# Phase 1 of an adaLN block on one Trainium2 core: the transpose of x moved from TensorE to DMA and GpSimd, for token pairs 2 to 7

## The chip, the core and the metric

The kernel runs as one launch on one core of a Trainium2 chip. The core has a matrix engine (TensorE; PE in the profile, with its weight loads listed apart as PEld), three engines for elementwise work (VectorE or DVE, ScalarE or ACT, GpSimd or POOL), a queue engine that only starts transfers (SyncE or SP), and 16 DMA engines that all queues share. Every engine works through its own list of instructions in order, and engines wait for one another at semaphores. The metric is the time of one execution on the device in microseconds (us).

## The reference

The reference is one transformer block with adaptive layer norm, float32, sequence 2048, width 640, 32 heads of 20, hidden width 1728:

```python
mod = (_silu(c) @ w_mod).reshape(1, 6, 1, -1)
sa, ca, ga, sb, cb, gb = (mod[:, i] for i in range(6))
h = _layernorm(x) * (1 + ca) + sa
q, k, v = split(h @ wqkv)
phi(u) = concat(softmax(u @ w_phi), softmax(-(u @ w_phi)))       # per head, u = q or k
o = phi(q) @ (phi(k).T @ v) / (phi(q) @ sum(phi(k)) + 1e-6)
x = x + ga * (o @ wo)
h = _layernorm(x) * (1 + cb) + sb
x = x + gb * (relu(h @ w1 + b1) ** 2 @ w2 + b2)
```

## The kernel before

**Tiles and phases.** The 2048 tokens are 16 tiles of 128, taken as 8 pairs: pair j holds tiles 2j and 2j+1. Phase 1 makes k, v and q of every tile and sums phi(k)ᵀv; phase 2 forms the attention output and multiplies by `wo`; phase 3 is the two-layer feed-forward part. The change is in phase 1 alone.

**What a pair needs.** A projection contracts over the 640 features, so the normalized x of a pair must stand with features on partitions: five columns of 128 features (`d` = 0 to 4), each 128 partitions by 256 tokens. `ln_parts` normalizes the pair in place in its tile `xb` in three steps, between which it yields: sums (ScalarE, two passes, and a small GpSimd operation), squares (ScalarE, two passes into the scratch rows `junk`, and three small GpSimd operations), and scaling (ScalarE, two passes). Then `t1` turns the columns: two TensorE transposes of 128 by 128 per column into the PSUM tile `ta` (`t_in`), and `t_out`: ScalarE applies the modulation to give `hf`, ScalarE copies `hf` rounded to the high part of `hT`, and VectorE subtracts to give the low part. Every float32 product is made of three rounded ones, high by high, high by low, low by high (`three`). So a column is usable by its first two matmuls once ScalarE has written the high part, and by its third once VectorE has written the low part.

**One pair on TensorE.** For each tile: the projection to k (30 matmuls: 15 into a 384-wide bank, then 15 into a 256-wide one, columns 0 to 4 in order in each), to v, to q. At the even tile, after v, `do_kv` adds the products of the two tiles before. The turning of pair j+1 is spread over pair j: columns 0 and 1 at the end of the even tile (`t1(j + 1, 0, 1)`), columns 2 and 3 after v of the odd tile, and column 4 inside the q projection of the odd tile, where for three pairs a transpose for the modulation vectors (`mod_turn`) also stands. The k projection of the next pair follows at once. Tiles 12 to 15 have no q projection in this loop, so the last pairs are close together: pair 6 is first used at tile 12.

**What sets the order.** In this loop only TensorE's order is written by hand (`manual_schedule(engines={PE})`). The lists of ScalarE, VectorE, GpSimd and SP come out of a scheduler that estimates when operands will be there; `issue_after` adds single constraints. The order so made is fixed in the program. The list of SP holds the loads of x (`load_x`), the rows of `w_mod` (`wm`) and `wo` (`rwo`), and the stores `esp` of each tile's exponentials of q.

**Shared buffers.** `row("s3", ...)` gives rows from three buffers in turn: `junk` of the squares and `hf` of every column come from it. Four banks of PSUM (`pj`) hold the projections, two per projection, so TensorE can run about one projection ahead of ScalarE's copies out of PSUM. The rows k and q come from two buffers (`s2`).

Of the kernel before, what the change touches and what calls it, by code (L numbers as in the profile page):

```python
# [9 lines left out]
F32R = mybir.dt.float32r  # L10
I32 = mybir.dt.int32
AF = mybir.ActivationFunctionType
ALU = mybir.AluOpType
AX = mybir.AxisListType

P = 128
# [5 lines left out]
NT = S // P  # L22
NC = D // P
# [28 lines left out]
def kernel(  # L52
# [19 lines left out]
    nc = tc.nc  # L72
# [258 lines left out]
    def ln_parts(xt, nm, spare=None):  # L331
# [15 lines left out]
        for i in range(2):  # L347
            nc.scalar.activation(xt[:, i], xt[:, i], AF.Identity, bias=nb[:, i : i + 1], scale=sq[:, i : i + 1])
        yield

    def layer_norm(xt, nm, spare=None):
# [30 lines left out]

    def t1(j, *ds, more=None):
        if 0 in ds:
            HT[j] = ht(f"hT{j}", j)
        p = tp(f"ta{j}_{ds[0]}")
        for k, d in enumerate(ds):
            t_in(XB[j], d, p[:, 256 * k : 256 * k + 256])
        if more:
            mod_turn(more[0], p[:, 256:], 4)  # L390
        for k, d in enumerate(ds):
            t_out(cols_a, HT[j], d, f"a{j}", p[:, 256 * k : 256 * k + 256])
        DONE[:] = newest(ET_.Activation), newest(ET_.DVE)
        if more:
            mod_sum(*more)
# [317 lines left out]
    for t in range(2, NT - 2):  # L713
# [8 lines left out]
        if norm:  # L722
            if not i:
                parts = ln_parts(XB[norm], f"a{norm}")
            with tc.issue_after(newest(ET_.Activation)):
                next(parts)
        p = proj("v", t, (1, 0, lambda: t1(j + 1, 4)) if t == NT - 3 else None)
        if i == 0:
            do_kv(t - 2)
            do_kv(t - 1)  # L730
            if t in AFTER_KV:
                AFTER_KV[t]()
        v_out(t, p)
        if norm and not i:
            next(parts)
        EK[t] = tok2("k", f"ek{t}")
        spread(PK[t], EK[t], f"k{t}")
        exps(EK[t])
        if norm and not i:
            next(parts)  # L740
        if i and t < NT - 4:
# [3 lines left out]
        if t < NT - POSTPONED:  # L745
            do_q(t, (1, 3, lambda: t1(j + 1, 4, more=LAST_COL.get(t))) if i else None)
            if norm and i:
                with tc.issue_after(newest(ET_.Activation)), tc.issue_after(DONE[0]):
                    next(parts)
            if i:  # L750
# [4 lines left out]
        if i == 0 and t < NT - 4:  # L755
            t1(j + 1, 0, 1)
        if t == NT - 6:
            parts = ln_parts(XB[j + 2], f"a{j + 2}")
            with tc.issue_after(newest(ET_.Activation)):
                next(parts)  # L760
# [942 lines left out]
```

## Time and profile before

| | |
|---|---|
| median of the runs (lowest, highest) | 766.53 us (766.48, 767.01) |
| profiled execution, its own time | 766.05 us |
| its span | 764.3 us |
| TensorE matmuls busy | 758.5 us (99%) |
| TensorE weight loads busy | 739.7 us (97%) |
| VectorE, ScalarE, GpSimd busy | 593.9, 435.6, 144.9 us |
| granted TensorE clock | 1.0 throughout |
| phase 1's loop over tiles 2 to 13 | about 52 to 224 us |

The profile's page gives busy time by engine; the chain that ended last follows the work back from the last instruction; groups give count, busy time and mean length by line and operand names; windows give the engines' busy time in a stretch; the timeline lists instructions by start, with what ended the idle time before them. Line numbers are those of the kernel before (L357 is `t_in`, L368 and L369 are `hf` and the high part of `hT`, L88 the subtraction, L337, L342 and L348 are sums, squares and scaling, L338 and L343 to L345 GpSimd's small operations).

### The profile page before, as it was taken

Reading aid. Unit: us, or ns where it says so; the run is one execution under the profiler, and the core shown is the slowest. Engines: PE = TensorE matmul, PEld = TensorE weight load, DVE = VectorE, ACT = ScalarE, POOL = GpSimd, SP = SyncE. Lnnn points to the kernel's source line nnn. Section 1 sums busy time; section 2 is a strip of 40 time slices with the busy share of each in tenths; the row PEclk is TensorE's granted clock in tenths of the full one; section 3 lists DMA queues with packets and bytes.
Section 4 is the critical chain, followed back from the end, with each engine's and each line's share of the span. In section 5 each row is a group of like instructions: output and inputs, shape, how many; then the busy total and the mean of one; then the engine's idle time right before and its main releaser. Section 6 shows DMA issues by size and latency. Waiting matters only on the chain.

```text
span 764.3 us, 15303 instructions
## 1 busy us (share of the span) xinstructions
PE 758.5 (99%) x5968; PEld 739.7 (97%) x5968; DVE 593.9 (78%) x1083; ACT 435.6 (57%) x972; POOL 144.9 (19%) x301
## 2 busy tenths in 40 slices
PE   9999999999999999999999999999999999999997
PEld 8999999999999989988999999999999999999997
DVE  6598897988999899999655667876767666685666
ACT  5766756677853364546776647465563645536331
POOL 3001101001100255432101000231321313213110
PEclk9999999999999999999999999999999999999999
DMA  8811431343332345223366466996766759767460
GB/s 322 329 61 78 138 104 54 104 136 112 126 104 93 109 150 188 72 87 104 122 194 221 120 227 236 283 334 209 224 166 207 232 179 268 199 184 204 126 184 35
DMA packets 51505, 126.69 MB, mean 166 GB/s; under 512 B 6684, under 2 KB 7457, under 8 KB 51433
## 3 DMA queue, kind: packets, MB, share of 16 engines
q1 hardware_dynamic: 34098, 84.65, 32.8%
q0 software_dynamic: 14752, 35.76, 16.9%
q10 hardware_dynamic: 2583, 5.30, 1.8%
q8 instruction: 47, 0.77, 0.5%
q14 instruction: 25, 0.20, 0.1%
HBM read 95.70 MB, written 29.89 MB: 164 GB/s over the span
## 4 chain that ended last, share of the span: by engine, by line
PE 91%; DVE 7%; DMA 1%; issue 0%; SPq 0%; ACT 0%; DVEq 0%
PE up L78 24%; PE acc L78 18%; PE pq L78 9%; PE pk L78 9%; PE pv L78 9%; PE pwo L78 6%; PE acc3x L78 5%; PE kvp L450 3%; PE te L920 1%; DVE dn L878 1%; DVE scr L876 1%; DVE ezb L900 1%; PE tb L357 1%; PE ta L357 1%; DVE ot L88 1%; PE foldq L280 1%
## 5 line engine op out<-in xcount | busy, mean ns | idle before, releaser
L78 PE MATMUL up<-h,w 128*128 128x256 f32 x1640 | 206.4, 278 | 0.0
L78 PEld LDWEIGHTS up<-h,w 128*128 128x128 f32 x1640 | 196.1, 188 | 0.0
L1255 ACT ACTIVATE ft<-up,b_t 128x256 f32<-128x256 f32 x104 | 49.1, 472 | 113.8 <-PE up L78 113.2
L78 PE MATMUL acc<-w,ra 128*128 128x384 f32 x452 | 97.4, 335 | 0.0
L1256 DVE TENSOR_TENSOR ft<-ft 128x256 f32<-128x256 f32 x104 | 44.1, 424 | 48.4 <-ACT ft L1255 46.8
L78 PE MATMUL pwo<-wo,ot 128*128 128x256 f32 (+3 forms) x512 | 80.5, 312 | 0.1
L78 PEld LDWEIGHTS pwo<-wo,ot 128*128 128x128 f32 (+1 forms) x512 | 74.4, 188 | 3.2 <-issue 2.7
L78 PE MATMUL pq<-wq,hT 128*128 128x384 f32 (+1 forms) x480 | 75.2, 312 | 0.0
L78 PEld LDWEIGHTS acc<-w,ra 128*128 128x128 f32 x452 | 72.7, 188 | 0.8 <-DVE ra L88 0.5
L78 PE MATMUL pk<-wk,hT 128*128 128x384 f32 (+1 forms) x480 | 72.7, 308 | 0.0
L78 PE MATMUL pv<-wv,hT 128*128 128x384 f32 (+1 forms) x480 | 71.7, 307 | 0.0
L78 PEld LDWEIGHTS pq<-wq,hT 128*128 128x128 f32 x480 | 71.1, 188 | 0.6 <-issue 0.2
L78 PEld LDWEIGHTS pk<-wk,hT 128*128 128x128 f32 x480 | 70.5, 188 | 0.4 <-issue 0.2
L78 PEld LDWEIGHTS pv<-wv,hT 128*128 128x128 f32 x480 | 70.1, 188 | 0.0
L88 DVE TENSOR_TENSOR ra<-ft,ra 128x384 fp32r<-128x384 f32 (+2 forms) x86 | 36.8, 449 | 32.6 <-ACT ra L1279 19.3
L1365 POOL DMA_DIRECT2D ring_a<-td_a x34 | 18.3, 539 | 126.1 <-PE acc L78 100.4
L1279 ACT ACTIVATE ra<-ft 128x384 fp32r<-128x384 f32 x48 | 25.2, 526 | 28.4 <-DVE ft L1256 22.4
L78 PE MATMUL acc3x<-w,ra 128*128 128x256 f32 x231 | 39.8, 278 | 0.0
L78 PEld LDWEIGHTS acc3x<-w,ra 128*128 128x128 f32 x231 | 37.2, 188 | 0.2 <-DVE ra L88 0.2
L1270 DVE TENSOR_TENSOR ft<-ft 128x128 f32<-128x128 f32 x136 | 33.4, 287 | 1.2
L441 DVE TENSOR_REDUCE sk<-ek 128x64 f32<-128x1280 f32 x16 | 23.7, 1484 | 12.4 <-ACT ek L436 10.8
L884 POOL TENSOR_TENSOR dn<-dn,rs_q 128x32 f32<-128x32 f32 x32 | 20.2, 630 | 66.7 <-DVE dn L878 66.4
(270 smaller groups left out, 1412.6 us busy)
## 6 DMA issues: line engine op xcount, KB each, us to landing
ring_c<-td_c POOLq DMA_DIRECT2D x34, 384.0 KB, 4.2
ring_a<-td_a POOLq DMA_DIRECT2D x34, 384.0 KB, 4.1
ring_b<-td_b POOLq DMA_DIRECT2D x34, 256.0 KB, 4.0
esp<-eq SPq DMA_DIRECT2D x12, 640.0 KB, 3.0
el<-esp SPq DMA_DIRECT2D x12, 640.0 KB, 3.9
rw<-in_w SPq DMA_DIRECT2D x23, 320.0 KB, 2.9
wm<-in_w_mod SPq DMA_DIRECT2D x20, 320.0 KB, 3.3
xb<-in_x SPq DMA_DIRECT2D x8, 640.0 KB, 4.2
```

The costliest lines, as they stand in the source:

```text
L78: nc.tensor.matmul(o, a, b, start=first and i == 0, stop=last and i == len(terms) - 1, skip_group_check=skip,)
L88: (eng or nc.vector).tensor_tensor(out_lo, full, hi.bitcast(F32), op=ALU.subtract)
L280: nc.tensor.matmul(p[g // 3][:, (g % 3) * 120 : (g % 3) * 120 + n], r, bd_t[:120, g * 120 : g * 120 + n], start=True, stop=True,)
L357: nc.tensor.transpose(p[:, i * P : (i + 1) * P], xn[:, i, d * P : (d + 1) * P], ident)
L441: nc.vector.tensor_reduce(s, heads(flat(e)), axis=AX.X, op=ALU.add)
L450: nc.tensor.matmul(kvp[g // 4][64 * c : 64 * c + 64, a : a + 2 * n].rearrange("p (s n) -> p s n", s=2), v[:, u], e[:, :, o : o + n], start ...
L884: nc.gpsimd.tensor_tensor(dn[:, s], dn[:, s], rs[:, 1 - s], op=ALU.mult)
L1255: nc.scalar.activation(r, p, AF.Relu, bias=b1_t[:, f : f + 1])
L1256: nc.vector.tensor_tensor(r, r, r, op=ALU.mult)
L1270: nc.vector.tensor_tensor(t[:, o], t[:, a], t[:, b], op=op)
L1279: nc.scalar.activation(a[:, 0, :3], t[:, :3], AF.Copy)
L1365: nc.gpsimd.dma_start(RING[j, n, r], TD[n][r].bitcast(F32R))
```

## The change

For pairs 2 to 7 the TensorE transposes of `t1` go. In their place `by_dma`, called at the end of the scaling step, treats the pair's tile as 16-bit halves: GpSimd copies (`tensor_copy`, every second 16-bit element) make for each of the two token tiles a plane `pl` of low halves and one of high halves, four copies of 128 by 640; the two planes of a token tile lie in one `s3` row. SP then starts four transposing transfers (`dma_start_transpose`), one for each plane, which write back over the tile `xb`. In `t1` GpSimd joins the two halves of a column, two strided copies of 128 by 256, into the row `hf`; from there `t_out` goes on as before, with `hf` in SBUF in place of `ta` in PSUM. Every edit follows from this but two: the transpose of `mod_turn` stands ahead of the columns and has a PSUM tile of its own, and the steps of `ln_parts` are called earlier in the program text (for pairs 3 to 6 the sums at the end of the odd tile before, the squares after k of the even tile, the scaling before the copies of v).

```diff
         for i in range(2):
             nc.scalar.activation(xt[:, i], xt[:, i], AF.Identity, bias=nb[:, i : i + 1], scale=sq[:, i : i + 1])
+        if nm[0] == "a":
+            by_dma(int(nm[1:]), xt)
         yield
+
+    TURNED = {}
+
+    def by_dma(j, xt):
+        raw = flat(xt).bitcast(U16)
+        halves = raw.rearrange("p (i d h) -> p i h d", i=2, h=2)
+        turned = raw.rearrange("p (h b t) -> p h b t", h=2, b=NC)
+        planes = [row("s3", f"pl{j}_{i}").bitcast(U16).rearrange("p (h d) -> p h d", h=2) for i in range(2)]
+        for i in range(2):
+            for h in range(2):
+                nc.gpsimd.tensor_copy(planes[i][:, h], halves[:, i, h])
+        for i in range(2):
+            for h in range(2):
+                nc.sync.dma_start_transpose(turned[:, h, :, i * P : i * P + P], planes[i][:, h])
+        TURNED[j] = turned
...
     def t1(j, *ds, more=None):
+        if more:
+            mod_turn(more[0], tp(f"mc{j}")[:, 256:], 4)
         if 0 in ds:
             HT[j] = ht(f"hT{j}", j)
-        p = tp(f"ta{j}_{ds[0]}")
-        for k, d in enumerate(ds):
-            t_in(XB[j], d, p[:, 256 * k : 256 * k + 256])
-        if more:
-            mod_turn(more[0], p[:, 256:], 4)
-        for k, d in enumerate(ds):
-            t_out(cols_a, HT[j], d, f"a{j}", p[:, 256 * k : 256 * k + 256])
+        for d in ds:
+            hf = row("s3", f"hfa{j}_{d}")[:, :256]
+            for h in range(2):
+                nc.gpsimd.tensor_copy(hf.bitcast(U16).rearrange("p (t h) -> p h t", h=2)[:, h], TURNED[j][:, h, d])
+            t_out(cols_a, HT[j], d, f"a{j}", hf, hf)
...
         if norm:
-            if not i:
+            if t == 2:
                 parts = ln_parts(XB[norm], f"a{norm}")
+                next(parts)
             with tc.issue_after(newest(ET_.Activation)):
                 next(parts)
...
                 AFTER_KV[t]()
+        if norm:
+            next(parts)
         v_out(t, p)
-        if norm and not i:
-            next(parts)
...
         exps(EK[t])
-        if norm and not i:
-            next(parts)
...
-            if norm and i:
-                with tc.issue_after(newest(ET_.Activation)), tc.issue_after(DONE[0]):
-                    next(parts)
...
-        if t == NT - 6:
+        if (i and t < NT - 5) or t == NT - 6:
             parts = ln_parts(XB[j + 2], f"a{j + 2}")
             with tc.issue_after(newest(ET_.Activation)):
                 next(parts)
```

Since the scheduler sets the lists of the other engines, the change moves more than its lines say. Three places follow; in the names the first number is the pair (`hT6`, `hfa6_2` is column 2 of pair 6) or the tile (`q11`, `pq11_1` its second bank).

ScalarE, before, at the end of tile 11, ahead of pair 6's first use at tile 12:

```order
L426 ACTIVATE q11_2562<-pq11_0_2520 128x384
L306 ACTIVATE mt4_2313<-ta6_4_2540 128x128
L368 ACTIVATE hfa6_4_2545<-ta6_4_2540,cols_a_100 128x256
L369 ACTIVATE hT6_2389<-hfa6_4_2545 128x256
L426 ACTIVATE q11_2562<-pq11_1_2521 128x256
L348 ACTIVATE xb7_2215<-xb7_2215,nba7_2405,sqa7_2404 128x640 x2
L426 ACTIVATE k12_2577<-pk12_0_2578 128x384
```

The same place after:

```order
L444 ACTIVATE q11_2612<-pq11_1_2571 128x256
L387 ACTIVATE hT6_2429<-hfa6_1_2436 128x256
L338 ACTIVATE xb7_2251,sma7_2442<-xb7_2251 128x640 x2
L518 ACTIVATE wo2_2452<-rwo2_2448 128x640
L343 ACTIVATE junka7_0_2491,sqa7_2443<-xb7_2251,sma7_2442 128x640
L343 ACTIVATE junka7_1_2493,sqa7_2443<-xb7_2251,sma7_2442 128x640
L349 ACTIVATE xb7_2251<-xb7_2251,nba7_2444,sqa7_2443 128x640 x2
L386 ACTIVATE hfa6_2_2554<-hfa6_2_2554,cols_a_100 128x256
L387 ACTIVATE hT6_2429<-hfa6_2_2554 128x256
L386 ACTIVATE hfa6_3_2560<-hfa6_3_2560,cols_a_100 128x256
L387 ACTIVATE hT6_2429<-hfa6_3_2560 128x256
L386 ACTIVATE hfa6_4_2593<-hfa6_4_2593,cols_a_100 128x256
```

Before, all five columns of pair 6 are written ahead of the copy of the second q bank; now columns 1 to 4 stand behind it, and columns 2 to 4 also behind all three steps of pair 7's normalization and a piece of the `wo` weights.

GpSimd, before, at pair 7's normalization:

```order
L489 MEMSET rwo4_2718 128x640
L338 TENSOR_SCALAR sma7_2403<-sma7_2403 128x2
L343 TENSOR_SCALAR sqa7_2404<-sqa7_2404 128x2
L344 TENSOR_TENSOR sqa7_2404<-sqa7_2404,mhalf_96 128x2
L345 TENSOR_TENSOR nba7_2405<-sma7_2403,sqa7_2404 128x2
L503 DMA wo5_2820<-wo5_2820 40x640
```

The same place after:

```order
L339 TENSOR_SCALAR sma7_2442<-sma7_2442 128x2
L344 TENSOR_SCALAR sqa7_2443<-sqa7_2443 128x2
L345 TENSOR_TENSOR sqa7_2443<-sqa7_2443,mhalf_96 128x2
L346 TENSOR_TENSOR nba7_2444<-sma7_2442,sqa7_2443 128x2
L363 COPY pl7_0_2532<-xb7_2251 128x640 x2
L363 COPY pl7_1_2533<-xb7_2251 128x640 x2
L409 COPY hfa6_2_2554<-xb6_1885 128x256 x2
L409 COPY hfa6_3_2560<-xb6_1885 128x256 x2
L409 COPY hfa6_4_2593<-xb6_1885 128x256 x2
```

The joins of pair 6's columns 2 to 4 stand behind the four splits of pair 7. The rows `hfa6_3` and `hfa6_4` also take the `s3` buffers of `pl7_0` and `pl7_1`, so their joins wait until pair 7's transposing transfers have read these planes.

ScalarE, before, around the q projection of tile 5, ahead of pair 3's first use at tile 6:

```order
L436 ACTIVATE ek5_1421<-ek5_1421 128x640
L437 ACTIVATE ek5_1421<-ek5_1421 128x640
L426 ACTIVATE q5_1485<-pq5_0_1446 128x384
L368 ACTIVATE hfa3_4_1469<-ta3_4_1466,cols_a_100 128x256
L369 ACTIVATE hT3_1330<-hfa3_4_1469 128x256
L426 ACTIVATE q5_1485<-pq5_1_1447 128x256
```

The same place after:

```order
L444 ACTIVATE q5_1499<-pq5_0_1461 128x384
L386 ACTIVATE hfa3_0_1348<-hfa3_0_1348,cols_a_100 128x256
L444 ACTIVATE q5_1499<-pq5_1_1462 128x256
L387 ACTIVATE hT3_1347<-hfa3_0_1348 128x256
L386 ACTIVATE hfa3_1_1354<-hfa3_1_1354,cols_a_100 128x256
L387 ACTIVATE hT3_1347<-hfa3_1_1354 128x256
L386 ACTIVATE hfa3_2_1445<-hfa3_2_1445,cols_a_100 128x256
L387 ACTIVATE hT3_1347<-hfa3_2_1445 128x256
L386 ACTIVATE hfa3_3_1451<-hfa3_3_1451,cols_a_100 128x256
L387 ACTIVATE hT3_1347<-hfa3_3_1451 128x256
L386 ACTIVATE hfa3_4_1481<-hfa3_4_1481,cols_a_100 128x256
L387 ACTIVATE hT3_1347<-hfa3_4_1481 128x256
```

Before, four columns are done ahead of the q projection's copies and the fifth between them; now the high parts of all five stand behind the copy of the second q bank. In the other pairs the columns whose high part stands behind that copy are 3 and 4 (pair 2), 2 to 4 (pair 4), and 1 to 4 (pair 5); of pair 7 none. On SP the four transposing transfers of pairs 3 and 5 are parted after the second by the store of the even tile's exponentials of q; those of the other pairs follow one another. On VectorE the low parts of the columns stand ahead of the odd tile's row sums of exp(k) and its q work.

More of the change, by code (lines that the diff above doesn't have):

```diff
@@ L11 @@
 I32 = mybir.dt.int32
+U16 = mybir.dt.uint16
 AF = mybir.ActivationFunctionType
```

## The prediction

> **What bounds the kernel now.** I read the page's busy times first, then windows by stage, then the chain inside phase 1.
>
> ```profile
> PE 758.5 (99%) x5968; PEld 739.7 (97%) x5968; DVE 593.9 (78%) x1083; ACT 435.6 (57%) x972; POOL 144.9 (19%) x301
> ...
> 82.00:112.00 30.00, 30.00 (x237) 29.78 (x236) 27.01 (x36) 19.75 (x45) 2.84 (x4) 1.00 0.35 114
> 203.00:232.00 29.00, 29.00 (x231) 28.75 (x230) 27.30 (x37) 16.66 (x37) 0.00 (x0) 1.00 0.32 110
> 232.00:253.00 21.00, 21.00 (x196) 20.10 (x197) 19.64 (x23) 7.97 (x20) 0.77 (x1) 1.00 0.32 99
> 253.00:350.00 97.00, 96.69 (x716) 86.52 (x713) 93.51 (x138) 49.34 (x111) 44.02 (x88) 1.00 0.38 125
> ```
>
> The windows give PE, PEld, DVE, ACT and POOL in this order. In phase 1 (the first two rows) TensorE never stops and loads weights 99% of the time, so what leaves its list is won, and what it waits for is lost. VectorE is busy 27.0 of 30 us. From 253 to 350 us VectorE is the fuller one (93.5 of 97), so a delay handed to it there isn't made up.
>
> The chain through one pair (tiles 4 and 5, from 81.95 to 111.77) is TensorE alone:
>
> ```profile
> 81.95 4.30 PE pk L78 x30
> 93.03 4.58 PE pq L78 x30
> 97.60 0.44 PE ta L357 x4
> 98.04 4.38 PE pk L78 x30
> 106.72 0.43 PE ta L357 x4
> 107.16 2.98 PE pq L78 x18
> 110.13 0.22 PE ta L357 x2
> 110.35 1.42 PE pq L78 x12
> ```
>
> **Part 1, the transposes removed.** 0.44 + 0.43 + 0.22 = 1.09 us of the path in each pair, 6.5 us in six. The groups bound it from above:
>
> ```profile
> L357 PEld LDWEIGHTS ta<-ident,xb 128*128 128x128 f32 x60 | 7.0, 141 | 0.1
> L357 PE MATMUL ta<-ident,xb 128*128 128x128 f32 x60 | 9.5, 273 | 0.0
> ```
>
> I take the chain's 6.5; the matmuls' 9.5 overlap their neighbours and are the upper end. `mod_turn`'s transposes only move.
>
> **Part 2, the columns of hT arrive late.** TensorE wants all five columns when the q projection of the odd tile ends; call that moment T. By ScalarE's list they now stand behind the copy of the second q bank, which can't begin before T. The durations:
>
> ```profile
> 98.99 0.72 ACT L369 ACTIVATE hT<-hfa 128x256 fp32r<-128x256 f32 x2
> 111.80 0.39 ACT L426 ACTIVATE q<-pq 128x256 f32<-128x256 f32 x1 [0.36 <-PE pq L78]
> 201.72 0.56 ACT L368 ACTIVATE hfa<-ta,cols_a 128x256 f32<-128x256 f32 x1
> 202.31 0.42 ACT L369 ACTIVATE hT<-hfa 128x256 fp32r<-128x256 f32 x1
> 202.83 0.41 DVE L88 TENSOR_TENSOR hT<-hfa,hT 128x256 fp32r<-128x256 f32 x1
> ```
>
> The copy begins 0.05 after T, and the next instruction 0.45 after T. From `hf` to its `hT` 0.59 passes, from `hT` to the next instruction 0.36 (two in 0.72): 0.95 for a column. From the start of `hT` until VectorE has the low part 0.52 + 0.41 = 0.93. TensorE uses column 4's low part in its 15th matmul, 14 × 0.166 = 2.3 us after T (2.98 for 18). So with columns n to 4 behind the copy, the last low part is there at 0.45 + 0.36 + (4 − n − 1) × 0.95 + 0.59 + 0.93 for n below 4, and the wait is what exceeds 2.3:
> - pair 2 (n = 3): 2.33, no wait. Pair 4 (n = 2): 3.28, 1.0 us. Pair 5 (n = 1): 4.2, 1.9 us. Pair 3 (n = 0): 5.2, 2.9 us.
>
> In pairs 3 and 5 the last two transposing transfers also stand on SP behind a store that waits for exponentials:
>
> ```profile
> 93.25 1.74 ACT L348 ACTIVATE xb<-xb,nba,sqa 128x640 f32<-128x640 f32 x2 [0.95 <-POOL nba L345]
> ...
> 105.07 0.33 SPq L480 DMA_DIRECT2D esp<-eq  x1
> 143.91 0.38 SPq L328 DMA_DIRECT2D gate<-gate_a  x1
> 154.18 0.34 SPq L329 DMA_DIRECT2D ga_b<-gate  x1
> ...
> xb<-in_x SPq DMA_DIRECT2D x4, 640.0 KB, 4.0
> ...
> rwo<-in_wo SPq DMA_DIRECT2D x10, 150.0 KB, 2.6
> ```
>
> No row shows a transposing transfer. It moves 160 KB in short pieces. Low end: 2.6 us to landing, as the 150 KB loads. High end: the column of 4-byte pieces (`gate`), whose reader went out 10.3 us later. I take 5.0, nearer the low end because the bytes are those of the low row, and above the 640 KB row because four follow one another. The last of them goes out at 105.07 + 2 × 0.33 and lands at 110.75; a join (below) ends at 111.15. T is now 111.77 − 1.09 = 110.68, so the first `hf` begins about 0.5 after T. That adds 0.85 in pair 3 (its `hf` stands ahead of the copy: 0.5 + 0.46, copy, 1.30 for the first `hT` in place of 0.45) and 1.8 in pair 5, where a whole column and another `hf` stand there (2.25 for 0.45). Sum of pairs 2 to 5: 0 + 3.75 + 1.0 + 3.7 = 8.5 us.
>
> In the other pairs scaling ends at 95.0 and the splits (0.9 each, below) at 98.6, so the transfers go out 12 us ahead of T; the odd tile's three projections (4.3 each) hide them, GpSimd's splits and the first joins. With transfers over 12 us that cover is gone.
>
> **Part 3, pair 6.** Behind T stand pair 7's sums, a `wo` piece, squares and scaling, then GpSimd's four splits, pair 7's transfers and pair 6's joins.
>
> ```profile
> 190.56 0.73 ACT L337 ACTIVATE xb<-xb 128x640 f32<-128x640 f32 x1
> 191.28 0.73 ACT L337 ACTIVATE xb<-xb 128x640 f32<-128x640 f32 x1
> 192.00 0.48 ACT L426 ACTIVATE k<-pk 128x384 f32<-128x384 f32 x1
> 193.70 0.82 ACT L342 ACTIVATE junka<-xb,sma 128x640 f32<-128x640 f32 x1
> 194.51 0.82 ACT L342 ACTIVATE junka<-xb,sma 128x640 f32<-128x640 f32 x1
> 195.32 0.73 ACT L500 ACTIVATE wo<-rwo 128x640 fp32r<-128x640 f32 x1
> 195.95 0.73 ACT L437 ACTIVATE eq<-eq 128x640 f32<-128x640 f32 x1
> 203.21 1.72 ACT L348 ACTIVATE xb<-xb,nba,sqa 128x640 f32<-128x640 f32 x2
> ...
> L338 POOL TENSOR_SCALAR sma<-sma x6: 217/226/579, 58.4 to 192.2; 128x2 f32<-128x2 f32 x6
> L343 POOL TENSOR_SCALAR sqa<-sqa x6: 192/396/658, 61.3 to 195.5; 128x2 f32<-128x2 f32 x6
> L344 POOL TENSOR_TENSOR sqa<-sqa,mhalf x6: 708/710/1362, 61.5 to 195.8; 128x2 f32<-128x2 f32 x6
> L345 POOL TENSOR_TENSOR nba<-sma,sqa x6: 240/600/1971, 62.3 to 196.6; 128x2 f32<-128x2 f32 x6
> L489 POOL MEMSET rwo<- x5: 627/632/637, 152.8 to 188.7; 128x640 f32 x5
> ```
>
> After T, in us (the POOL rows give shortest, median and longest in ns): copy and column 1's `hT` to 0.8; two sums of 0.72 to 2.25; the `wo` piece 0.63 to 2.9; two squares of 0.81 to 4.5; GpSimd's three small operations, medians 0.40 + 0.71 + 0.60 and handovers, 2.2, to 6.7; scaling 0.86 each, the first done at 7.6. No row shows GpSimd copying. Low end for a split: the 0.63 of the MEMSET, as wide and without a read; high end 1.97, the longest small operation beside VectorE. I take 0.9, near the MEMSET, for VectorE is mostly held at this place. A join is 0.4 (0.226 for 2 columns, 0.632 for 640, interpolated at 256); a row of 640 that grew as the split would make it 0.5. Splits end at 11.2, the transfers of the two planes go out complete at 10.7 and 11.3 and land at 15.7 and 16.3. Column 3's joins end at 16.5, column 4's at 17.3; then 0.59 + 0.93 gives 18.8, less 2.3: a wait of 16.5 us. In pair 7 nothing stands between and TensorE works 20 us from its k to the first use.
>
> **Part 4, VectorE.** It stands in front of column 2's low part for that time with the odd tile's work queued behind, and comes out 1 to 3 us later against TensorE than before (sums of exp(k) stood before T, now after). Its spare time to 253 us is 1.7 + 1.4 us in the windows above, so between 0 and 2.8 us is lost; I take 1.5.
>
> **The sum**, made on the profiled execution (766.05 us, span 764.3; the median is 0.5 more): 766.05 − 6.5 + 8.5 + 16.5 + 1.5 = 786.05, forecast 786.
>
> **Rules of the Trainium skill.** "VectorE: DVE Perf Modes", section The three transpose paths, lists 1309 ns for a 128×128 16-bit block turned by DMA; "DMA: Bandwidth & Descriptors", section Latency and other measured facts, lists 261 GB/s for a transposing transfer. An estimate by the first is 6.5 us for the five blocks of a transfer and 26 us for a pair's four in a row, by the second 0.6 us each; by the first the total would lie between rivals 1 and 2, by the second some 5 us below the sum. No run shown here holds such a transfer.
>
> **Rivals.**
> 1. *The transposing transfers are slow but overlap*: 10.3 us each, the `gate` row. Adds 5.3 in each of pairs 3, 5 and 6: 802 us. For it: short pieces. Against: every other row of transfers lands within 4.
> 2. *They are slow and follow one another*: 41 us for a pair, 29 past the 12 of cover, in five pairs: over 900 us.
> 3. *GpSimd's copies stop VectorE*. Per pair 4 × 0.9 + 10 × 0.4 = 7.6 us, of which VectorE can spare 3.0 (27.0 of 30). In pairs 2, 4 and 7, which have no long wait to hide it, 4.6 each: 800 us. For it: the same tiny operation takes 240 to 1971 ns; against: that shows GpSimd waiting, not VectorE. The skill's "GPSIMD Engine Reference", section Specifications, says that GpSimd's SBUF interfaces are shared with VectorE.
> 4. *Pair 6's delay is partly made up*: TensorE's weight loads fill 86.5 of 97 us from 253 on, so up to 10 us could be absorbed if VectorE's work weren't delayed with it: 776 us.
> 5. *The columns are ready in time* (the other side): if ScalarE ran pair 6's columns ahead of T, only part 1 would be left: 766.05 − 6.5, about 760 us. It decides where all waits come to less than 6.5 us. Against: at the lowest prices (splits 0.63, transfers 2.6, small operations 1.5) pair 6 alone waits 13 us, and the list is fixed.
>
> **How the numbers follow.** Forecast 0.52; rival 1 0.25; rival 2 0.06; rival 3 0.07; rival 4 0.07; rival 5 0.03. About 0.2% (1.5 us) is what can be told from no change. Faster is rival 5, 0.03; the same, 0.01, is the tail of rival 4; slower 0.96. Low end: 9.5 won, 5.8 lost in pairs 2 to 5, 13 in pair 6: about 775, less 2 for pieces of rival 4: 773. High end 818: rivals 1 and 3 with one another. Left out are rivals 2 and 5 and edges, under 0.2.
>
> **What would show it.** Right: no `ta` transposes for pairs 2 to 7; TensorE idle ahead of `pk` at tiles 6, 8 and 10 by 1 to 4 us and at tile 12 by some 16, ended by ScalarE's or VectorE's `hT`; transposing transfers landing in 3 to 8 us; phases 2 and 3 as long as before. Wrong: landings over 10 us, waits at tile 4, VectorE's operations growing longer beside GpSimd's copies, or a wait at tile 12 under 10 us.

## The result, and the profile after

The changed kernel takes 794.66 us (793.67 to 795.40) against 766.50 for the kernel before, run on the same chip: a ratio of 1.0365 with a 95% interval of 1.0349 to 1.0380. The forecast was 786, its range 773 to 818. The profiled execution took 794.8 us with a span of 793.1, 28.8 more than the 764.3 before.

The page of the changed kernel, its busy times, the granted clock in 40 slices of 19.8 us, and GpSimd's joins (line 409 is the join, 363 the split, 366 the transposing transfer, 386 and 387 `hf` and the high part of `hT`, 89 the subtraction, 459 to 461 `k_norm`):

```profile
PE 763.8 (96%) x5908; PEld 737.1 (93%) x5908; DVE 598.6 (75%) x1083; ACT 437.3 (55%) x972; POOL 197.0 (25%) x385
...
PEclk9999998999959999999999999999999999999999
...
L409 POOL COPY hfa<-xb 128x256 uint16<-128x256 uint16 x60 | 37.0, 670 | 46.7 <-DMA xb<-pl 27.5
```

TensorE has sixty matmuls fewer to do and takes 29 us longer; its busy share fell from 99% to 96%. The waits of TensorE between 40 and 260 us (before the change this list is empty) give us in total, times, and the longest:

```profile
PE pk L79 <- ACT hT L387: 15.7, 6, 9.7
PE pk L79 <- DVE hT L89: 6.8, 8, 1.5
```

All of it is the k projection waiting for a high part (ScalarE) or a low part (VectorE) of `hT`. The splits, the transfers and their landing, from the rows by line (shortest, median, longest):

```profile
L363 POOL COPY pl<-xb x24: 714/716/1974, 60.5 to 222.6; 128x640 uint16<-128x640 uint16 x24
...
L366 SPq DMA_TRANSPOSE xb<-pl x24: 1199/1226/1655, 61.9 to 225.9; - x24
...
DMA to landing us min/median/max: 2.6/2.6/4.6
```

A transfer holds SP for 1.2 us and has landed 2.6 us after its issue (the trace has the landing of five of the 24; four took 2.6, one 4.6).

To place the loss I use one measure for each even tile from 4 to 12 (the first use of pairs 2 to 6): from the end of the q projection ahead (T) to the first matmul of v, less the 4.14 us that a k projection takes there when nothing is missing. Before, it is 0.0 at tiles 4 to 10 and 0.4 at tile 12 (two transposes stand there). After, it is 0.9, 6.9, 2.9, 4.4 and 19.0. With 1.2 us in which v itself ran slower at tile 6 that is 35.3, and v of tile 12 begins 28.55 later than before (235.93 against 207.38), so some 6.7 us had been won up to there by the transposes that went. Pair 7's other transposes win 0.6 more: k of tile 14 begins 27.9 later (251.71 against 223.80), which makes 7.4 won in all. At the end of phase 2 it is still 27.85, and phase 3 adds 0.9.

Tile 6 and tile 12 on TensorE, with the granted clock (the column ahead of the last two in the windows):

```profile
105.68 4.46 PE L79 MATMUL pq<-wq,hT 128*128 128x384 f32 x30
110.92 2.49 PE L79 MATMUL pk<-wk,hT 128*128 128x384 f32 x8 [0.78 <-ACT hT L387]
114.90 1.47 PE L79 MATMUL pk<-wk,hT 128*128 128x384 f32 x6 [1.49 <-DVE hT L89]
117.49 3.89 PE L79 MATMUL pk<-wk,hT 128*128 128x384 f32 x16 [1.13 <-DVE hT L89]
121.18 5.62 PE L79 MATMUL pv<-wv,hT 128*128 128x384 f32 x30
...
211.16 1.66 PE L79 MATMUL pq<-wq,hT 128*128 128x256 f32 x12
...
225.27 1.33 PE L79 MATMUL pk<-wk,hT 128*128 128x384 f32 x3 [9.65 <-ACT hT L387]
229.45 2.32 PE L79 MATMUL pk<-wk,hT 128*128 128x384 f32 x5 [2.85 <-ACT hT L387]
232.24 3.89 PE L79 MATMUL pk<-wk,hT 128*128 128x384 f32 x16 [0.47 <-DVE hT L89]
235.93 4.67 PE L79 MATMUL pv<-wv,hT 128*128 128x384 f32 x30
```

v of tile 12 before:

```profile
207.38 4.56 PE L78 MATMUL pv<-wv,hT 128*128 128x384 f32 x30
```

The clock after:

```profile
114.00:117.00 3.00, 1.47 (x6) 0.94 (x6) 2.97 (x5) 1.02 (x2) 0.61 (x1) 0.94 0.82 230
117.00:120.00 3.00, 2.51 (x11) 2.51 (x12) 3.00 (x5) 0.49 (x1) 0.00 (x0) 0.50 0.59 208
120.00:124.00 4.00, 4.00 (x18) 4.00 (x18) 3.92 (x6) 2.58 (x6) 0.00 (x0) 0.56 0.04 18
...
231.00:236.00 5.00, 4.53 (x19) 4.02 (x20) 4.97 (x9) 2.09 (x5) 1.27 (x4) 0.50 0.55 184
```

The last 16 matmuls of k took 3.89 us in both places; at the full clock they take 2.15. So part of the loss is not waiting but running behind a wait with a granted clock of 0.50.

### The profile page after: what moved, and what is told of

Same layout as the page of the kernel before. It is cut to its first block, busy times and chain, and to the rows that moved or that the text cites. A ratio compares the mean times of both kernels' runs of the same rounds, so it can differ in the third digit from the quotient of the medians.

```text
span 793.1 us, 15366 instructions
## 1 busy us (share of the span) xinstructions
PE 763.8 (96%) x5908; PEld 737.1 (93%) x5908; DVE 598.6 (75%) x1083; ACT 437.3 (55%) x972; POOL 197.0 (25%) x385
## 4 chain that ended last, share of the span: by engine, by line
PE 68%; DVE 16%; DMA 5%; ACT 4%; issue 4%; POOL 3%; SPq 1%; POOLq 0%; DVEq 0%; ACTq 0%
PE up L79 21%; PE acc L79 15%; PE pv L79 7%; PE pk L79 6%; PE pq L79 5%; PE acc3x L79 4%; PE pwo L79 4%; DVE dn L892 2%; DVE scr L890 2%; DVE ezb L914 2%; PE kvp L468 2%; DMA xb<-pl 1%; PE tb L375 1%; DVE sk L459 1%; DMA raw_q<-in_wq 1%
## 5 line engine op out<-in xcount | busy, mean ns | idle before, releaser
L79 PE MATMUL pk<-wk,hT 128*128 128x384 f32 (+1 forms) x480 | 82.7, 326 | 22.8 <-ACT hT L387 15.7
L79 PEld LDWEIGHTS pk<-wk,hT 128*128 128x128 f32 x480 | 73.3, 199 | 31.0 <-ACT hT L387 18.7
L409 POOL COPY hfa<-xb 128x256 uint16<-128x256 uint16 x60 | 37.0, 670 | 46.7 <-DMA xb<-pl 27.5
L89 DVE TENSOR_TENSOR hT<-hfa,hT 128x256 fp32r<-128x256 f32 x40 | 17.5, 445 | 30.8 <-ACT hT L387 28.0
```

What stands on the lines that cost most here:

```text
L79: nc.tensor.matmul(o, a, b, start=first and i == 0, stop=last and i == len(terms) - 1, skip_group_check=skip,)
L89: (eng or nc.vector).tensor_tensor(out_lo, full, hi.bitcast(F32), op=ALU.subtract)
L409: nc.gpsimd.tensor_copy(hf.bitcast(U16).rearrange("p (t h) -> p h t", h=2)[:, h], TURNED[j][:, h, d])
```

## The experiments

The waits by tile, in us, by the measure above, read from one profiled execution of each kernel; the medians are of all its executions. Slower matmuls within k count as wait by this measure. The kernels are in the order of the text.

| kernel | tile 4 | 6 | 8 | 10 | 12 | median, us | ratio to before (95%) |
|---|---|---|---|---|---|---|---|
| after | 0.9 | 6.9 | 2.9 | 4.4 | 19.0 | 794.7 | 1.0365 (1.0349, 1.0380) |
| steps alone | 0.0 | 0.0 | 0.0 | 0.0 | 0.4 | 767.7 | 1.0019 (1.0009, 1.0028) |
| turn alone | 3.5 | 4.9 | 4.3 | 2.1 | 7.2 | 786.5 | 1.0251 (1.0232, 1.0270) |
| transfers twice | 6.5 | 6.9 | 7.9 | 7.8 | 24.5 | 813.2 | 1.0607 (1.0591, 1.0622) |
| pair 7's sums ahead | 0.9 | 6.9 | 3.0 | 4.5 | 17.8 | 793.3 | 1.0352 (1.0336, 1.0368) |
| pair 7 by TensorE | 0.9 | 5.7 | 3.9 | 4.4 | 8.5 | 785.5 | 1.0243 (1.0224, 1.0262) |
| waits filled | 0.9 | 5.6 | 6.4 | 5.4 | 21.4 | 796.7 | 1.0391 (1.0373, 1.0408) |
| all steps sooner | 3.9 | 4.4 | 4.7 | 5.0 | 6.4 | 788.8 | 1.0290 (1.0275, 1.0306) |
| columns placed sooner | 1.6 | 4.9 | 5.1 | 1.9 | 18.5 | 792.6 | 1.0354 (1.0333, 1.0376) |
| both sooner | 1.6 | 0.0 | 0.0 | 1.5 | 0.7 | 774.2 | 1.0102 (1.0087, 1.0117) |
| both, pair 7 by TensorE | 1.6 | 0.0 | 0.0 | 1.5 | 1.8 | 767.4 | 1.0012 (1.0004, 1.0021) |
| the same, scaling tied | 1.6 | 1.5 | 0.9 | 3.1 | 2.3 | 770.5 | 1.0056 (1.0043, 1.0068) |
| pairs 2, 5, 7 by TensorE | 1.2 | 0.0 | 0.0 | 0.7 | 0.4 | 768.7 | 1.0030 (1.0019, 1.0041) |

The theory I began with: the loss is the order of the lists. ScalarE's columns stand behind the copy that begins at T, VectorE has other work between the low parts, pair 7's work stands ahead of pair 6's columns. The rivals: the transfers are too slow, or GpSimd's copies stop VectorE.

### One half of the change at a time

The steps alone (TensorE turns as before):

```diff
-        if nm[0] == "a":
-            by_dma(int(nm[1:]), xt)
...
-        for d in ds:
-            hf = row("s3", f"hfa{j}_{d}")[:, :256]
...
+        p = tp(f"ta{j}_{ds[0]}")
+        for k, d in enumerate(ds):
+            t_in(XB[j], d, p[:, 256 * k : 256 * k + 256])
```

> Edit: the new times of sums, squares and scaling are kept, and the turning is TensorE's again, as before the change (no planes, transfers or joins). The queue theory says that the columns stand on ScalarE where they stood before, ahead of or between the two copies of q, so that nothing waits: 765 to 769, against 766.5 before. If the earlier ScalarE steps cost something themselves (they are squeezed between the copies of k and the exponentials), this kernel is slower than 770. The rival of slow transfers says 766.5 too, so this run tells only whether the moved steps have a share.

Measured 767.7, no wait at any of the five tiles (the 0.4 at tile 12 are the two transposes, as before). The moved steps cost about 1.3 us; T of tile 12 is 1.05 later than before.

The turn alone (the loop over tiles 2 to 13 calls the steps of `ln_parts` where they stood before the change):

> Edit: the turning by transfers is kept, and sums, squares and scaling stand where they stood before the change. The queue theory: three columns a pair (2, 3 and 4) stand behind the second copy of q on ScalarE in pairs 2 to 5, which is 3 to 5 us each; pair 6 has pair 7's squares (1.7 us) ahead of three columns, so 5 to 7; minus 6.5 us of TensorE transposes taken away: 773 to 786. If it was the transfers' own length that cost the time, this kernel is slower than the changed one (its transfers start later): over 797.

Measured 786.5, just above the upper edge of what the queue theory gave; the four waits of pairs 2 to 5 come to 14.8. So the turn by transfers makes the columns late wherever the steps stand, and the moved steps don't make them on time. At tile 12 the wait is only 7.2: with the old steps pair 7's scaling, and so its splits, comes after pair 6's columns. But then pair 7 is late itself: k of tiles 14 and 15 takes 5.1 us longer than before the change, which the table doesn't show.

### The transfers, doubled

```diff
-        for i in range(2):
+        for i in [0, 1, 0, 1]:
             for h in range(2):
                 nc.sync.dma_start_transpose(turned[:, h, :, i * P : i * P + P], planes[i][:, h])
```

> Edit: each of the four transposing transfers of a pair is issued twice, with the same source and destination; the program is otherwise the changed kernel's. It adds 4 issues of 1.2 us on SyncE, so the last landing of each pair comes 4.9 us later. The queue theory reads the landings against the end of TensorE's work ahead of k: in pair 4 they land some 9 us ahead of it, so nothing changes there; in pairs 3 and 5 the last landing is within 3 us of it, and 2 to 5 us each are added. Pairs 3 to 5 together: +3 to +9. (Pair 6's instructions stand in another order in this program, that of the kernel with pair 7's sums sooner, so the whole time may be below 794.7; the comparison is by pair.) The rival that the transfers' length sets every wait says +4.9 in each of pairs 3, 4 and 5.

Measured 813.2, and neither theory has the pattern: against the changed kernel tile 4 waits 5.6 longer, tile 6 as long as before, tile 8 4.9 longer, tile 10 3.4 and tile 12 5.6. The edit also costs more than planned. SP's list in pair 4, first of the changed kernel and then of this one, with GpSimd's first join of this one:

```profile
130.97 5.18 SPq L366 DMA_TRANSPOSE xb<-pl  x4
```

```profile
137.70 12.91 SPq L366 DMA_TRANSPOSE xb<-pl  x8
...
150.75 0.86 POOL L409 COPY hfa<-xb 128x256 uint16<-128x256 uint16 x2 [11.75 <-DMA xb<-pl]
```

Eight issues hold SP for 12.9 us, 7.7 more where 4.9 was planned; why isn't shown (a transfer that waits for one under way to the same destination would be one reason). Pair 4's joins then begin at 150.8, 0.7 ahead of T (151.42), where in the changed kernel three of the five columns were joined 6.6 us ahead of it (140.7 and 147.30). So the transfers' time is hidden in pair 4 with a few us to spare, and where it isn't hidden it is a part of the chain; the list of ScalarE is not all of it. That tile 6 waits as long as before is chance: the last low part comes 1.2 us later after T than in the changed kernel, and the clock, which fell sooner here, takes as much less of the last 16 matmuls (2.63 for 3.89).

### Pair 6: what stands ahead of its columns

```diff
-        if i == 0 and t < NT - 4:
-            t1(j + 1, 0, 1)
         if (i and t < NT - 5) or t == NT - 6:
             parts = ln_parts(XB[j + 2], f"a{j + 2}")
             with tc.issue_after(newest(ET_.Activation)):
                 next(parts)
+        if i == 0 and t < NT - 4:
+            t1(j + 1, 0, 1)
```

> Edit: pair 7's sums stand in the program ahead of pair 6's columns 0 and 1 instead of behind them; nothing else. The theory of the queue's order says that in the changed kernel pair 7's sums and squares (four ScalarE instructions and the three small GpSimd ones behind them, together some 5 us from 214.6 to 219.6) run in the wait at tile 12 and nothing else needs them there. With them ahead, only pair 7's scaling and its four splits on GpSimd stay in front of pair 6's joins for columns 2 to 4: the wait there falls from 19.0 to 6 to 9 us, and the time from 794.7 to 781 to 786. The rival of slow transposing transfers says that the time stays within 1 us of 794.7, since the transfers are the same and land in the same order; so does the rival that GpSimd's copies stop VectorE.

A miss: 793.3, and the wait at tile 12 fell by 1.2, not by 11. The sums and squares did go ahead of T. GpSimd and SP in this run:

```profile
219.35 1.43 POOL L409 COPY hfa<-xb 128x256 uint16<-128x256 uint16 x2
226.36 0.85 POOL L409 COPY hfa<-xb 128x256 uint16<-128x256 uint16 x2 [5.59 <-DMA xb<-pl]
```

```profile
220.92 5.17 SPq L366 DMA_TRANSPOSE xb<-pl  x4
```

The join of pair 6's column 3 waited 5.6 us for a transposing transfer, and the only ones under way are pair 7's, issued from 220.92. It doesn't need their data: its row is one of the three of `s3`, and pair 7's planes hold two of them until they have been read. My expectation had left out this link, which the prediction's part 3 had. The next run takes it away:

```diff
-        if nm[0] == "a":
+        if nm[0] == "a" and nm != "a7":
             by_dma(int(nm[1:]), xt)
...
+        if j == 7:
+            p = tp(f"ta{j}_{ds[0]}")
+            for k, d in enumerate(ds):
+                t_in(XB[j], d, p[:, 256 * k : 256 * k + 256])
+            for k, d in enumerate(ds):
+                t_out(cols_a, HT[j], d, f"a{j}", p[:, 256 * k : 256 * k + 256])
```

> Edit: pair 7 alone is turned by TensorE again; pairs 2 to 6 and all steps stay. In the run with pair 7's sums sooner the join of pair 6's column 3 was released by pair 7's transfer, since its buffer is one of the three that pair 7's planes take. The theory is now: the wait at tile 12 is set by pair 7's splits and transfers standing ahead of pair 6's joins in that ring of three buffers, and pair 7's sums and squares (3.4 us of ScalarE) are the small part of it. Without pair 7's planes and transfers, ScalarE's order up to the squares is the changed kernel's, and the wait at tile 12 falls from 19.0 to 6 to 8; ten transposes come back (1.1): 781 to 785. If the ring is not the cause, and ScalarE's sums, squares and what the scheduler puts there are, it stays over 790.

785.5 (just above the range given), and the wait at tile 12 fell from 19.0 to 8.5 (in the profiled execution, which took 783.0). Pair 7's splits and transfers, ahead of pair 6's joins, are 10.5 of the 19.0. The run takes their place in GpSimd's list and in the ring of three rows away together; in the changed kernel's trace the list holds the join of column 2 until the splits are done (223.29), and the ring that of column 3 until a transfer has landed (227.46).

### The clock behind a wait

```diff
+    FILL = {6: 32, 12: 100}
+
+    def fill(t):
+        w, p = W["k", 0], tp(f"fill{t}")
+        for _ in range(FILL[t]):
+            nc.tensor.matmul(p[:, :384], w[:, 0, :P], w[:, 0, :384], start=True, stop=True)
...
-        to_sb(proj("k", t), PK[t])
+        to_sb(proj("k", t, (0, 0, lambda: fill(t)) if t in FILL else None), PK[t])
```

> Edit: the changed kernel with work added: 32 matmuls of a weight by itself into an unused bank ahead of k at tile 6 (about 5.5 us at the full clock) and 100 at tile 12 (about 17 us), so that TensorE runs while it would wait there; their result is not used. If the waits' cost includes a slower clock behind them (0.50 granted around 117 to 124 and 219 to 236), it goes: k and v of tiles 6 and 12 run at their usual 2.15 for the last 16 matmuls and 4.46, and 3 to 5 us come back although nothing is computed sooner: 789.5 to 792. If the clock is not what slowed them, the time stays at 794.7 or rises by what the added matmuls run over (up to 3). Tiles 8 and 10 are left as they are (the order of ScalarE's instructions at tile 8 differs a little, which may move its wait by 1 to 2).

At tile 6 it came out as the clock theory said. TensorE there in this run:

```profile
109.36 5.72 PE L437 MATMUL fill<-wk 128*128 128x384 f32 x32
114.91 4.53 PE L79 MATMUL pk<-wk,hT 128*128 128x384 f32 x30
119.28 4.46 PE L79 MATMUL pv<-wv,hT 128*128 128x384 f32 x30
```

With the same columns at the same times, k and v run at their usual length, and 2.5 us come back (1.3 of the wait, 1.2 of v). The whole time rose to 796.7, which by itself lies in the range that I had given for a clock without a part in it: the added bank moved ScalarE's list, tile 8 waits 3.5 more (half of it a clock of 0.50 there, which the changed kernel did not have at this tile), and at tile 12 the added matmuls themselves began 2.2 late and ran past the columns (their 100 took 19.2 us). So the run shows the clock's part at tile 6 and not at tile 12.

### Steps, places, and both

The steps all sooner (for pairs 3 to 7 sums and squares in the odd tile two ahead, scaling right behind k's copies of the even tile); the columns' places stay:

```diff
+        if i and t <= NT - 5:
+            parts = ln_parts(XB[j + 2], f"a{j + 2}")
+            with tc.issue_after(newest(ET_.Activation)):
+                next(parts)
...
         v_out(t, p)
+        if i and t <= NT - 5:
+            next(parts)
```

> Edit: sums and squares of pairs 3 to 7 stand in the odd tile two ahead of the pair's first (behind k's copies and behind v's copies), pair 7's scaling at the end of tile 11, the other scalings right behind k's copies of the even tile; the columns' places in the program are the changed kernel's. The theory of order: the transfers of a pair are issued half a tile sooner, so that columns 0 to 3 stand on ScalarE ahead of the second copy of q in pairs 4 and 5, ahead of or between in pair 6, and only column 4 (and a scaling of the next pair) behind it. The waits at tiles 6, 8, 10, 12 fall from 6.9, 2.9, 4.4, 19.0 to 0.5 to 2.5 each; tile 4 (pair 2, whose three columns stand behind the copy now) may rise from 0.9 to 3.5. 765 to 773. The rival that transfers or GpSimd's copies slow the rest by their own length, wherever they stand, says that most of the 28 stays: over 785.

A miss: 788.8, which is in the range given for the rival that transfers and copies cost their own length. At tile 12 it won 12.6, but tiles 4, 8 and 10 wait longer than in the changed kernel, and v of tile 9 another 2.1. The lists decide between that rival and the order. ScalarE and VectorE at tile 8 (T is 147.65):

```profile
148.65 1.73 ACT L349 ACTIVATE xb<-xb,nba,sqa 128x640 f32<-128x640 f32 x2
150.28 0.42 ACT L387 ACTIVATE hT<-hfa 128x256 fp32r<-128x256 f32 x1
```

```profile
148.45 1.48 DVE L459 TENSOR_REDUCE sk<-ek 128x64 f32<-128x1280 f32 x1
149.96 0.55 DVE L460 RECIPROCAL sk<-sk 128x64 f32<-128x64 f32 x1
150.55 1.81 DVE L461 TENSOR_TENSOR ek<-ek,sk 128x1280 f32<-128x1280 f32 x1
152.28 0.93 DVE L89 TENSOR_TENSOR hT<-hfa,hT 128x256 fp32r<-128x256 f32 x1
```

Column 4 alone is late, and two things stand in front of it: the next pair's scaling (1.73) on ScalarE, and all of `k_norm` (3.8) on VectorE. The data was there (GpSimd had joined the last column by 145.9); its place in the lists wasn't.

The columns' place alone (2, 3 and 4 right behind v of the odd tile; with it goes the constraint that tied `k_norm` behind VectorE's newest instruction):

```diff
         v_out(t, p)
+        if i and t < NT - 4:
+            t1(j + 1, 2, 3, 4)
...
-        if i and t < NT - 4:
-            t1(j + 1, 2, 3)
-        with tc.issue_after(newest(ET_.DVE)):
-            k_norm(EK[t], t)
+        k_norm(EK[t], t)
```

> Edit: only the columns' place: columns 2, 3 and 4 stand in the program right behind the odd tile's copies of v, as in the best run so far; sums, squares and scaling stand as in the changed kernel. With the run that moved only the steps (788.8) and the one that moved both (774.2) this closes the square. The theory that a column must be both turned in time and placed in time: the transfers still land late, the scheduler still puts columns 2 to 4 behind the second copy of q in pairs 3 and 4, and pair 6 still shares the ring with pair 7's planes, so that hardly anything is won: 788 to 796. If the place in the program alone is what counts, it is near 774 to 780.

792.6, as expected. Both edits together:

> Edit: as the kernel with all steps sooner, and columns 2, 3 and 4 stand in the program right behind the odd tile's copies of v, not around q, since no TensorE instruction has to be fitted in for them; the short TensorE transpose of the modulation stays in q. The theory of order: all five columns of pairs 3 to 6 stand on ScalarE ahead of the first copy of q, joins of pair 6 ahead of the splits of pair 7 on GpSimd, so nothing waits at tiles 6, 8, 10 and 12 (under 0.3 each), the clock stays at full rate there, and tile 4 waits 1 to 3. 766.4 less 6.5 of transposes, plus 1 to 3 at tile 4, plus the 1.3 that the sooner steps alone were measured at: 761 to 766, faster than both kernels. The rival that GpSimd's copies and the transfers themselves delay VectorE and TensorE says over 775.

774.2, 8 above the range, but the waits are those expected: 1.6, 0.0, 0.0, 1.5, 0.7. One edit won 5.9, the other 2.0, both 20.4. Tile 12's v began at 205.81, 1.6 sooner than before the change; the rest went at tile 14, which I had taken for covered. SP's list parts pair 7's transfers: the splits were done at 209.0, but only the first transfer went out then (207.13), and the other three stood behind a store, from 211.87 on, so that GpSimd's first join began at 215.49. TensorE there, with a clock of 0.50 from about 227 to 237 behind the waits:

```profile
222.27 1.03 PE L79 MATMUL pk<-wk,hT 128*128 128x384 f32 x5
226.50 2.12 PE L79 MATMUL pk<-wk,hT 128*128 128x384 f32 x7 [3.20 <-DVE hT L89]
228.81 1.01 PE L79 MATMUL pk<-wk,hT 128*128 128x384 f32 x2 [0.19 <-ACT hT L387]
231.97 9.01 PE L79 MATMUL pk<-wk,hT 128*128 128x384 f32 x46 [2.16 <-DVE hT L89]
```

With pair 7 turned by TensorE besides (the edit is that of the run above):

> Edit: the kernel with steps sooner and columns placed behind v, and pair 7 turned by TensorE. In the run without the last of these, v of tile 12 began at 205.8, 1.6 sooner than before the change, and all of the loss (and more) came at tile 14, where pair 7's columns were late. With pair 7 turned as before the change, nothing of it should be late: the rest of the program then runs as before it, and the end comes 1 to 2 us sooner than before: 764 to 766 against 766.2. If instead GpSimd's copies and the fuller ScalarE hold the end of the phase back, it is over 768.

767.4, above the 764 to 766 expected, and 1.0012 of before with an interval of 1.0004 to 1.0021: 27.3 of the change's 28.2 us are back, and no more. The waits left (1.6, 1.5, 1.8 less the 0.4 that stood there before, and 1.1 in tile 9's q) come to some 5.6, most of what the 50 transposes less had won (some 6.3, by the 1.27 us that a pair's turning took on TensorE).

Two more edits at those waits. The scaling tied behind k's copies:

```diff
         if norm:
-            next(parts)
+            with tc.issue_after(newest(ET_.Activation)):
+                next(parts)
```

> Edit: as the run before it, but the scaling of pairs 3 to 6 is tied behind k's copies of the even tile instead of free to go ahead of them. It makes the transfers 2 us later and k's copies 2 us sooner. The theory of order: columns 3 and 4 of pairs 3 to 6 stand between or behind the copies of q, so tiles 6, 8, 10 and 12 wait 0.5 to 2 each: 765 to 771, slower than the free one by 1 to 5.

770.5, as expected: 2 us later for the transfers costs 0.9 to 1.6 us at each of tiles 6, 8 and 10. And pairs 2 and 5 turned by TensorE (`BY_PE = {2, 5, 7}` in place of 7 alone):

> Edit: as the kernel with steps sooner, columns behind v and pair 7 on TensorE, and pairs 2 and 5 are turned by TensorE as well, in the places that they had before the change; pairs 3, 4 and 6 alone are turned by transfers. In that kernel's trace tiles 6 and 8 wait for nothing, and the waits left are 1.6 at tile 4 (pair 2), 1.5 at tile 10 and 1.1 in q of tile 9 (pair 5), and 1.8 at tile 12, where 0.8 is pair 7's two transposes and the wait for its scaling. Turned by TensorE, pairs 2 and 5 cost 1.1 each instead of 1.6 and 2.6. If those waits are what is left between this kernel and a gain, it is 2.0 sooner: 764 to 766 against 766.4 before and 767.4 of that kernel. If something that every such kernel shares is left (the moved steps, or GpSimd's copies beside VectorE), it stays at 767 or more.

A miss: 768.7. The waits at tiles 4 and 10 did shrink, but the PSUM tile `ta` of pair 5's column 4 and the modulation's `mc` now share the one `tp` bank one after the other, and TensorE waited for it in tile 9's q:

```profile
172.25 0.33 PE L306 MATMUL mc<-ident,wm 128*128 128x128 f32 x1 [2.83 <-ACT hfa L386]
```

Without those 2.8 it would be near 766, but that wasn't run. No kernel here beats the one before.

## Why the prediction was right, and where its steps were off

The forecast of 786 is 8.7 low; sign, place and mechanism were right, and the size lies in the terms:

| step | forecast | measured |
|---|---|---|
| 1, transposes removed | −6.5 | −7.4 |
| 2, pair 2 | 0 | 0.9 |
| 2, pair 3 | 3.75 | 6.9 and 1.2 in v |
| 2, pair 4 | 1.0 | 2.9 |
| 2, pair 5 | 3.7 | 4.4 |
| 3, pair 6 | 16.5 | 19.0 |
| 4, VectorE's lag into phase 2 | 1.5 | 0.0 |
| phase 3, not in the sum | 0 | 0.9 |

**Part 1** holds, 0.9 too small: without its waits a pair (from T to T) is 1.27 us shorter than before (28.54 against 29.81), where the chain's pieces of the transposes gave 1.09.

**Part 2 is the step that failed**, by 7.8 us: it priced ScalarE's list and left out two things. The first is VectorE's own list. Between the low parts of pair 3 stand two multiply-adds for the modulation and the first half of `k_norm`:

```profile
111.91 0.63 DVE L89 TENSOR_TENSOR hT<-hfa,hT 128x256 fp32r<-128x256 f32 x1 [0.51 <-ACT hT L387]
112.46 1.83 DVE L297 SCALAR_TENSOR_TENSOR wm<-wm,cs,wm 128x640 f32<-128x640 f32 x2
114.21 0.96 DVE L89 TENSOR_TENSOR hT<-hfa,hT 128x256 fp32r<-128x256 f32 x2
115.10 1.47 DVE L459 TENSOR_REDUCE sk<-ek 128x64 f32<-128x1280 f32 x1
116.61 0.55 DVE L460 RECIPROCAL sk<-sk 128x64 f32<-128x64 f32 x1
117.08 0.36 DVE L89 TENSOR_TENSOR hT<-hfa,hT 128x256 fp32r<-128x256 f32 x1
```

The last low part was there at 117.44, 7.3 after T, where the step had 6.05. Nothing of that was a late transfer: `hf` of column 0 began at 108.92, ahead of T, so the 0.85 for it was not paid. A link that the step didn't have took its place, by chance of nearly the same size: the join of column 4 began when VectorE's subtraction of column 1 had given its row of `s3` back, and took 2.02 us beside VectorE instead of 0.86, so that ScalarE waited 0.93 for it.

```profile
112.60 2.02 POOL L409 COPY hfa<-xb 128x256 uint16<-128x256 uint16 x2 [0.28 <-DVE hT L89]
```

The second thing is the clock: of the 8.1 us at tile 6, 1.74 are the last 16 matmuls of k at a clock of 0.50 and 1.16 the slower v.

**Part 3** has the mechanism and nearly the size. Pair 7's scaling began 6.8 us after T (6.7 priced), the splits ended 10.5 after it (11.2), the join of column 3 began 14.6 after it (15.7):

```profile
219.66 1.73 ACT L349 ACTIVATE xb<-xb,nba,sqa 128x640 f32<-128x640 f32 x2 [1.38 <-POOL nba L346]
...
220.64 2.70 POOL L363 COPY pl<-xb 128x640 uint16<-128x640 uint16 x4 [1.02 <-ACT xb L349]
...
227.46 0.85 POOL L409 COPY hfa<-xb 128x256 uint16<-128x256 uint16 x2 [3.33 <-DMA xb<-pl]
```

The single prices were off in both directions: transfers 2.6 for 5.0, splits 0.68 for 0.9, joins 0.43 for 0.4. That the sum came near is in part luck: SP sends the transfers 1.3 us apart, where the prediction went by the 0.33 of a store, so the third, behind whose landing the join of column 3 began, went out only at 224.68. From the last split to this join 4.1 us passed, where 4.5 were priced for other reasons. The last low part came 19.4 after T for 18.8, since the first half of `k_norm` (2.0) again stood ahead of it, and the half clock added 1.7. The claim that pair 7 has room (20 us from its k to the first use) holds for the changed kernel but only because tile 12 is so late: in the run with both edits, pair 7 was what waited.

**Part 4** was counted in the wrong place. VectorE's queue did cost, within the waits of parts 2 and 3, and nothing after them: the delay is 27.9 at k of tile 14 and the same at the end of phase 2. The 0.9 of phase 3 has other causes; 0.44 of it is a wait of TensorE for a transfer of weights (`ring_a`, at 521.2), the rest stays open.

**The rivals.** Transfers of 10.3 us (rival 1) and transfers in a row (rival 2) are excluded by the landing of 2.6, at most 4.6. The Trainium skill's "VectorE: DVE Perf Modes", section The three transpose paths, has 1309 ns for a 128×128 block, which made an estimate of 6.5 for a transfer; the trace disagrees, with 2.6 from issue to landing for five blocks. That GpSimd's copies stop VectorE (rival 3) is seen in the traces, as slower instructions and not as a stop. VectorE's subtraction for q between 60 and 206 us, before and after:

```profile
L433 DVE TENSOR_TENSOR eq<-q,mxq 128x640 f32<-128x640 f32 x18 | 14.1, 814 | 0.0
```

```profile
L451 DVE TENSOR_TENSOR eq<-q,mxq 128x640 f32<-128x640 f32 x17 | 14.1, 869 | 0.0
```

That is 7% on this instruction; the low parts of `hT` grew by 12% in the same stretch (419 to 471 ns), while sums and maxima kept their length. The run with the steps alone, which has none of the copies, is at 810 ns again, so the growth comes with them. In the runs with both edits it is not so small: 1019 ns, 25% more than before, and what that adds to the waits left there was not tried apart. A join took 0.46 us at the least, 0.67 on the mean and 2.08 at the most. But as the cause of the loss the rival is out: in the run with both edits, with the same copies, tiles 6 and 8 waited for nothing. Rival 4 (pair 6's delay made up) didn't happen: the delay at tile 12 reached the end whole. Rival 5 (columns in time) is what the runs with both edits built, and even they only came level. The high end of the range, rivals 1 and 3 together, comes to 816 by their own prices and not 818; nothing hangs on it.

## What to carry to other kernels

When work leaves the engine that sets the order by hand, its place goes with it: the rest of the chain is then placed by a scheduler's own guess, and both the data's time and the consumer's place in every list behind it (here ScalarE's and VectorE's, and SP's for pair 7) have to be moved, since here either alone won little. Look in the same lists for what else stands between two pieces of one operand, and in the buffers' ring for who must give a row back first. Price a wait of a busy TensorE with the slower stretch behind it.

## What the runs showed of the hardware

The granted clock fell to 0.50 in pieces of about 3.4 us. How long it stayed there follows from the windows: what a window's mean clock lacks to 1.0, times its length, over 0.5. In the changed kernel around tile 6 it is (0.06 × 3 + 0.50 × 3 + 0.44 × 4) / 0.5 = 6.9 us, two pieces; around tile 12 17 us, five pieces. In the run with pair 7 by TensorE, which differs only in pair 7's turn, one piece:

```profile
114.00:117.00 3.00, 2.18 (x6) 1.67 (x6) 2.97 (x6) 1.02 (x2) 0.39 (x1) 0.64 0.88 252
117.00:120.00 3.00, 2.74 (x18) 2.74 (x19) 3.00 (x5) 0.60 (x2) 0.00 (x0) 0.80 0.53 188
```

That is (0.36 × 3 + 0.20 × 3) / 0.5 = 3.4 us, and it makes the two runs differ by 2.4 us at this one tile (wait and v together). With one piece or two from the same waits, such a stall has no single price. The Trainium skill's "TensorE: Matmul & The Clock Gate", Part 1, tells of a free-running window of 3413 ns in which TensorE's activity is watched; the pieces agree with it. The same page of the Trainium skill, section Why this matters for your kernels, warns of idle gaps above about 3 us; here shorter ones were enough. In the run with pair 7 by TensorE the drop began about 114.8, when only gaps of 0.78 and 1.49 us lay behind T, and in the changed kernel about 116.6, within a third of 1.13. The waits of 2.9 and 4.4 at tiles 8 and 10, also in pieces, brought no drop in the changed kernel. In the run with filled waits the same last three gaps at tile 10 (0.40, 0.42, 0.78) did; the last matmuls of k there, first in the changed kernel and then in that run:

```profile
185.85 2.17 PE L79 MATMUL pk<-wk,hT 128*128 128x384 f32 x16 [0.78 <-DVE hT L89]
```

```profile
186.04 3.64 PE L79 MATMUL pk<-wk,hT 128*128 128x384 f32 x16 [0.78 <-DVE hT L89]
```

So in these runs the gaps alone don't decide whether the clock falls.
